# Another table of the issue order in a kernel of attention and MLP on one core

## The chip, the core and the metric

The kernel runs on one core of a Trainium2 chip. The metric is the device time of one launch in microseconds (us). A core has five engines with queues of their own, each working through its instructions in order: TensorE (PE, matrix products), VectorE (DVE), ScalarE (ACT), GpSimd (POOL) and SyncE (SP, which only issues transfers here). DMA transfers are issued by SP and ACT.

## The reference, cut

Four batches of eight heads with 768 tokens of 64 elements go through block-sparse attention (blocks of 32; a query block sees its neighbours, the first and the last block and three sampled ones; the first and the last query block see all). The result, 3072 tokens of 512, goes through an MLP with a width of 2048.

```python
mask = np.abs(blk_i - blk_j) <= window
mask = mask | (blk_i == 0) | (blk_j == 0) | (blk_i == n_blocks - 1) | (blk_j == n_blocks - 1)
...
scores = np.where(mask, scores, -1000000000.0)
scores = scores - np.max(scores, axis=-1, keepdims=True)
attn = np.exp(scores)
attn = attn / (np.sum(attn, axis=-1, keepdims=True) + 1e-09)
return np.matmul(attn, v).astype(np.float32)
...
h = x @ w_in
sp = np.where(h > 20.0, h, np.log1p(np.exp(np.minimum(h, 20.0))))
g = h * np.tanh(sp)
return (g @ w_out).astype(np.float32)
```

## The kernel before, in words

**Products.** Values of 32 bits are split into a high and a low part of 16 bits, and a product is the sum of three: high by high, high by low, low by high. In the listings `kt`, `q`, `v`, `ph`/`pl`, `xh`/`xl`, `wi`, `wo`, `g` and `sg` are such parts. Scales that keep the low parts in range come from sums of squares, which PE forms (`gram_k`, `gram_q`, `gram_v`, `gram_wi`, `gram_wo`, L373) and DVE reads off (L388).

**Attention.** A job is a group of 128 query rows by head pairs; job 0 is dense (first query block, `t_0_0` to `t_0_2`), jobs 1 and following read gathered blocks. For a job PE forms the scores `s` (L674), DVE their maximum `mx` (L737), ACT the exponentials `pt` (L756), PE transposes them (`t`, L680), ACT cuts the high part `ph` (L779), PE subtracts it (`t`, L787), ACT or DVE cut the low part `pl` (L792, L783), and PE multiplies by the values into `obank` (L818). DVE takes the reciprocal `r` (L837) and writes `xs`; PE transposes that (`tx`), and `xh`, `xl` are the MLP's input. Sampled blocks of k are copied to `kg` (ACT L608, POOL L611, DVE L615), whose places are read into registers first. Values are written to a DRAM buffer `vd` (L553) and gathered from there into one of three tiles `vg0` to `vg2` by DMAs on SP (the fixed blocks L571, the window L628, L631, the sampled blocks L635), with register loads for their places (L580) on SP ahead of them.

**Weights.** w_in comes in eight pieces of 1 MB (`wr_0` to `wr_7`) and w_out in sixteen of half that (`wor_0` to `wor_15`), all issued by one line, L893, on ACT's queue or on SP's. A piece is decoded by DVE in three steps (L901, L904, L907) out of one of three buffers, which come free when the third step is done, then scaled by its gram, and split into high (L962 on ACT, L965 on DVE) and low parts (L968).

**MLP.** For each of twelve tiles of 256 tokens PE forms `h` (L1068). ACT scales it to `hs` (L1079), takes exp (L1098), the square (L1104, or POOL L1103), ln (L1105) and exp (L1106); DVE puts a min/add (L1101) behind the first and a multiply (L1107) behind the last, which gives g. Its parts are cut by ACT or DVE (high, L1114, L1116) and POOL or DVE (low, L1120, L1122). The first tiles go through `y` (L1162). For the late tiles sums of parts (`us` by L1133, `sg` high L1144 on ACT or L1146, low L1148) replace some products (`yr`, L1281), and the results are put together in `yz` (L1314, L1320).

**Order.** All work is recorded as 2703 tasks, many with two ways (two engines). `Plan.emit` then reads the text table `ORDER` from left to right: a word is a task's number, a letter b takes its second way, and +n puts n zeros ahead of it, dummy products of PE on constants (`neg`, L1506). Since each engine works in order, the table sets the order of every engine and queue. A DMA carries one of eight completion semaphores (DMAHW0 to DMAHW7 in the listings), and it waits, at the head of its issuing engine's queue, until the transfer that had the semaphore before has landed, if that isn't known yet; it also waits for the buffer that it fills. What stands behind it on that engine waits with it.

Of the kernel before, what the change touches and what calls it, by code (L numbers as in the profile page):

```python
# [219 lines left out]
def attn_mish_kernel(ctx: ExitStack, tc: tile.TileContext, qT, kT, v, sampled, blocks, w_in, w_out, out):  # L220
# [1338 lines left out]
    147 97 72 183 55 179 98 112 341b 88 185 102 186 46 113 129 103+7 47 104 48 187 105 106 58 188+1 205 107 84 114 63  # L1559
    206 189 207 190+8 121 201 194 148 191 209+2 208 108 153 343+2 210 149 109 211 115 363 344 365b 195 340 116 196 345  # L1560
    122 213+4 212 130 197 217+7 150 203 214 131 135 123 346 215 124 110 216 348 347 342 154 125 367 132 198 352 126
    133 59 236 218 349 199 134 91 368 353 350+9 127 151 364 354 219 351 155 369 220+3 224 356 355 389 152 221 87 357
    156 370 222 366 387b 358 157 372+2 136 223 158 137 373 371 68 374+4 359 128 260b 244 391+2 80 375 138 360 411 421b
    361 419 392 166 83 139+3 159 362 388 376+3 140 393 225 160 377 226 141 394 378 142 237 143 396+2 261 65 245 380
    238 397 71 246 379 412 86 264 144 398 381 390 399 239 395 227 145 400+1 382 423 165 401 240b 247 228 70 383 443
# [3 lines left out]
    456 484 1629 268b 506 439 1638 457 440 485 257 486 235 1640 243 248 487 1630 488 253 441 164 458 442 489 459 482  # L1569
    510 1631b 254 1639 1641 511 529 1632 460 527 81 512 289 491 490 1651 500 492 285 78 1633 269 493 507 461 1652 513  # L1570
    249 1634 1642 290 514 515 258 494 286 462 495 1653 509 255 531 1643 270 1654 259 1635b 250 463 516 528 1655 1636
    496 501 517 518 532 1665 519 591 1656 272b 520 533 276b 497 1657 1644 291 292 89 521 251 498 522 1645 530 534 499
    293 523 1666 535 271 536 1668 1658 537 280b 273 1646 548 1659 538 524 1669 525 1667 526 1647 287 294 539 593 1660
    1679 1648 540 1680 1661 541 1649b 1662 551 1670 542 1650 552 1663b 543 1684 550 1671 549 544 1664 1685 553 1681
    554 295 1697 274 555 281 277 1698 275 1686 1672 464 1687 556 278 559 1702 279 560 557 561 1673b 296 282 297 298
    1688 299 1699 562 283 1674 300 1703 1689 558 563 1675 564 301 302 303 545 1717 1676 546 465 547 565 1704 304 1677
    466 1678 305 588 1718 306 467 566 590 307 1722 309b 1690 308 1723 310 1719 1691 313b 468 1735 311 469 314 1724 502
    1736 317 503 318 504 1740 312 321 1692 315 1682 1705 322 316 1683 325 505 470 1741 319 326 570 320 329 1695 323
    330 1696 324 333 589 327 334 592 567 1700 328 337 331 338 595 1725 332 1701 596 614 335 594 568 336 597 1713 598
    611 569 615 634 1714 599 612 90 1706 571 600 473b 1715 603 617 1716 604 613 601 1720 1707 618 572 602 619 1721 573  # L1580
    476b 605 620 606 1726 471 1733 616 1727b 477b 574 472 1734 621 575 607 1708 622 625 623 1693 1738 626 624 1694
    1728 627 1739 474 608 1729 576 478 628 1737 1751 629 609 610 475 630 1752 631 1709 632 1755 580 1753b 1710 1742
    1758 584 1730 1711b 585 640 636 635 1756 581 641 1712 1731b 1760 1743 582 1759 642 1757 665 659 577 586 1761 1754
# [18 lines left out]
    917 925 932 896 966 1924 1899 897 935 1928 967 926 1914 918 1915 1929 891 1900 919 898 1926 887 1916 888 976 968
    1930 920 1917b 1006 1901 981 1918 1902 947 1927 982 1931 957 977 983 1945 892 1009 1932 1946 893 984 1906 889 1950
    894 1919 948 890 1941 985 1000 1920 2303 986 989 987 1012 990 988 1933 969 1029 1031 991 1951 1947 1013 979 1028
    980 1934 992 949 1942 950 970 993 1315 1001 1032 994 1963 951 1935b 1943 1002 1964 1014 1003 1008 1015 2304 1948
    1016 2305b 1952 971 1017 972 1949 1004 973 978 1953 1961 1936 1954 1020 1921 1955b 1034 1011 1922 995 1035 1962
# [104 lines left out]
```

## Time and profile before

| what | value |
|---|---|
| time, median of 3 runs | 754.28 us (751.87 to 755.23) |
| profiled execution, its own time | 754.41 us |
| its span | 752.6 us |
| PE busy | 708.4 us (94%), mean granted clock 0.984 |
| ACT busy | 579.3 us (77%) |
| DVE busy | 548.1 us (73%) |
| POOL busy | 281.7 us (37%) |
| chain that ended last | PE 82%, DVE 7%, DMA 4%, issue 3%, SP's queue 2% |

The shares are means over the whole span. The page's slices of 1/40 show PE at half to eight tenths in the first six and at nine tenths behind them, so the stretch at the start has to be read by itself. "X <- Y" with a time means that the instruction X stood idle for that time and that Y was seen to end last of what it waited for.

### The profile page before, as it was taken

Reading aid. Unit: us, or ns where it says so; the run is one execution under the profiler, and the core shown is the slowest. Engines: PE = TensorE matmul, PEld = TensorE weight load, DVE = VectorE, ACT = ScalarE, POOL = GpSimd, SP = SyncE. Lnnn points to the kernel's source line nnn. Section 1 sums busy time; section 2 is a strip of 40 time slices with the busy share of each in tenths; the row PEclk is TensorE's granted clock in tenths of the full one; section 3 lists DMA queues with packets and bytes.
Section 4 is the critical chain, followed back from the end, with each engine's and each line's share of the span. In section 5 each row is a group of like instructions: output and inputs, shape, how many; then the busy total and the mean of one; then the engine's idle time right before and its main releaser. Section 6 shows DMA issues by size and latency. Waiting matters only on the chain.

```text
span 752.6 us, 31176 instructions
## 1 busy us (share of the span) xinstructions
PE 708.4 (94%) x13023; PEld 543.4 (72%) x13023; DVE 548.1 (73%) x1015; ACT 579.3 (77%) x927; POOL 281.7 (37%) x380
## 2 busy tenths in 40 slices
PE   5567798999999999999999999999999999999997
PEld 4455577875776776777676776677677778888887
DVE  5869878897667856977767757877886855577665
ACT  2648677999796788887877789886887786787783
POOL 2004234517754551244543454564374301200140
PEclk9889899999999999999999999999999999999999
DMA  8788766533235273247337353344532447000001
GB/s 302 249 250 245 227 212 179 198 121 88 108 112 167 83 251 103 93 132 217 91 104 229 102 213 108 82 142 144 159 88 72 145 131 245 16 1 15 16 29 43
DMA packets 60050, 103.75 MB, mean 138 GB/s; under 512 B 8579, under 2 KB 20868, under 8 KB 59908
## 3 DMA queue, kind: packets, MB, share of 16 engines
q1 hardware_dynamic: 54576, 88.90, 37.9%
q10 hardware_dynamic: 5332, 12.85, 5.2%
q8 instruction: 102, 1.67, 0.9%
q14 instruction: 40, 0.33, 0.1%
HBM read 84.58 MB, written 17.14 MB: 135 GB/s over the span
## 4 chain that ended last, share of the span: by engine, by line
PE 82%; DVE 7%; DMA 4%; issue 3%; SPq 2%; ACT 1%; POOLq 0%; ACTq 0%; POOL 0%; DVEq 0%
PE h_None L1068 31%; PE y L1162 21%; PE yr L1281 8%; PE obank L818 6%; PE t L680 6%; PE s L674 5%; DMA vg<-vd 2%; PE obank L1281 1%; PE tx L680 1%; DMA raw_k<-in_k_dram 1%; DVE hs_None L1107 1%; DMA raw_q<-in_q_dram 1%; SPq L580 1%; DVE v L504 1%; ACT pt L756 1%
## 5 line engine op out<-in xcount | busy, mean ns | idle before, releaser
L1068 PEld LDWEIGHTS <-wi 128*128 128x128 f16 x2304 | 223.8, 98 | 38.6 <-issue 5.4
L1068 PE MATMUL h_None<-xh,wi 128*128 128x256 f16 x1152 | 208.1, 274 | 3.2 <-issue 3.2
L611 POOL COPY kg<-kt 128x256 f16 x246 | 112.5, 491 | 163.2 <-PE s L674 146.3
L1162 PE MATMUL y<-wo,g 128*128 128x512 f16 x672 | 159.1, 379 | 0.0
L1068 PE MATMUL h_None<-xl,wi 128*128 128x256 f16 x576 | 157.6, 274 | 0.0
L1120 POOL TENSOR_TENSOR g<-hs_None,g 128x1024 f16<-128x1024 f32 x36 | 81.0, 2251 | 131.3 <-ACT g L1114 85.7
L1162 PEld LDWEIGHTS <-g 128*128 128x128 f16 x768 | 74.1, 98 | 70.8 <-issue 1.1
L756 ACT ACTIVATE pt<-s,nb,ns 128x256 f32<-128x256 f32 (+1 forms) x208 | 107.4, 584 | 1.3 <-DVE wi L907 0.9
L779 ACT ACTIVATE ph<-t 128x512 f16<-128x512 f32 x112 | 66.1, 600 | 47.1 <-PE t L680 39.2
L783 DVE SCALAR_TENSOR_TENSOR pl<-t,ph 128x512 f16<-128x512 f32 x99 | 67.0, 684 | 35.0 <-ACT ph L779 34.8
L680 PE MATMUL t<-ident,pt 128*128 128x128 f32 x448 | 68.9, 280 | 9.3 <-ACT pl L792 4.4
L1107 DVE SCALAR_TENSOR_TENSOR hs_None<-us_None,hs_None 128x1024 f32<-128x1024 f32 x48 | 62.7, 1307 | 18.9 <-ACT us_None L1106 17.6
L1079 ACT ACTIVATE hs_None<-h_None,gsc 128x512 f32<-128x512 f32 x96 | 66.0, 687 | 13.6 <-PE h_None L1068 13.6
L737 DVE TENSOR_REDUCE mx<-s 128x4 f32<-128x1024 f32 x44 | 53.7, 1220 | 27.8 <-PE s L674 27.8
L1068 PE MATMUL h_None<-xr,wi 128*128 128x256 f16 x576 | 67.8, 273 | 0.0
L680 PEld LDWEIGHTS t<-ident,pt 128*128 128x128 f32 x448 | 52.3, 143 | 21.3 <-ACT pl L792 5.7
L818 PEld LDWEIGHTS <-ph 128*32 128x32 f16 x3584 | 47.8, 94 | 14.7 <-issue 12.9
L1098 ACT ACTIVATE us_None<-hs_None,hsc 128x1024 f32<-128x1024 f32 x48 | 55.4, 1154 | 1.6 <-DVE sg L1148 1.1
L818 PE MATMUL obank<-vg,ph 128*32 128x65 f16 (+1 forms) x3200 | 49.1, 196 | 2.6 <-issue 2.3
L1105 ACT ACTIVATE us_None<-us_None 128x1024 f32<-128x1024 f32 x48 | 50.9, 1059 | 0.3
L1106 ACT ACTIVATE us_None<-us_None 128x1024 f32<-128x1024 f32 x48 | 50.7, 1060 | 0.4
L818 PEld LDWEIGHTS <-pl 128*32 128x32 f16 x1792 | 46.5, 96 | 5.7 <-issue 3.8
(258 smaller groups left out, 1202.9 us busy)
## 6 DMA issues: line engine op xcount, KB each, us to landing
vg<-vd SPq DMA_DIRECT2D x320, 65.0 KB, 2.6
vg<-vd SPq DMA_DIRECT2D x80, 195.0 KB, 3.2
wr<-in_moe_w_in_dram ACTq DMA_DIRECT2D x7, 1024.0 KB, 6.3
vd<-v SPq DMA_DIRECT2D x12, 520.0 KB, 4.2
vg<-vd SPq DMA_DIRECT2D x12, 520.0 KB, 5.3
raw_k<-in_k_dram SPq DMA_DIRECT2D x12, 512.0 KB, 5.8
raw_q<-in_q_dram SPq DMA_DIRECT2D x12, 512.0 KB, 4.4
raw_v<-in_v_dram SPq DMA_DIRECT2D x12, 512.0 KB, 4.9
```

Of the source, the lines that this page charges most:

```text
L611: nc.gpsimd.tensor_copy(out=dst, in_=tl["kt", b][:, :, ds(j, BS)])
L680: nc.tensor.matmul(out, src, ident, start=start, stop=stop, is_transpose=True)
L756: ex = lambda o, x, g, w: nc.scalar.activation(out=o, in_=x, func=AF.Exp, bias=nb[:, g, w:w + 1], scale=tl["ns", b, sus[w]["qb"] // TB][:, ...
L779: nc.scalar.activation(out=new(at_, "ph", ("ph", i, j), [P, 2, 2, P], F16), in_=tl["t", i, j], func=AF.Copy, scale=PSC)
L783: nc.vector.scalar_tensor_tensor(out=new(at_, "pl", ("pl", i, j), [P, 2, 2, P], F16), in0=tl["t", i, j], scalar=PSC, in1=tl["ph", i, j], o ...
L818: nc.tensor.matmul(o[cs, w, g, 0:v1 - v0], p[:, k, g, cs], vt[:, k, 2 * c + g, v0:v1], start=j == 0 and g == 0 and k == 0 and n == 0, stop ...
L1068: nc.tensor.matmul(h[:, f2, 0:n].rearrange("p (s q) -> p s q", q=BS), wi[:, fp, w, cc, fs], x[:, s0:s0 + sn, cc], start=f2 == 0 and k == 0 ...
L1079: nc.scalar.activation(out=tl[kq][:, 2 * (fp % 2):2 * (fp % 2) + 2, 0:n], in_=tl[kh][:, :, 0:n], func=AF.Copy, scale=gsc[:, fp:fp + 1])
L1107: add("DVE", 1.32 * c, lambda: nc.vector.scalar_tensor_tensor(out=hs(), in0=us(), scalar=-0.5, in1=hs(), op0=ALU.add, op1=ALU.mult), r=[ku ...
L1120: add("POOL", 2.3 * c, lambda: nc.gpsimd.tensor_tensor(out=g(1), in0=hs(), in1=g(0), op=ALU.subtract), r=[kq, ("gh",) + kp], w=[kp], use=[kg],
L1162: nc.tensor.matmul(tl[ky], tl["g", b, t, k][:, g, f, q], wo_at(fc)[:, w], start=fc == 0 and n == 0, stop=fc == NFC - 1 and n == 2)
L1281: nc.tensor.matmul(R(i), lhs, rhs, start=head and j == n == 0, stop=k == NFC // 4 - 1 and j == 1 and n == 2, skip_group_check=True)
```

## The change

Only the text of `ORDER` differs. It names the same 2703 tasks in another sequence; 128 of its words have the letter b (117 before), and 120 zeros stand at 16 places (113 at 22 before). The largest group of zeros, ahead of task 172 (the first transposes `t_0_0`), has 51 (33 before); of those that stood ahead of it, 5 and 6, none is left. 83 tasks change their engine: fifteen weight loads go from ACT's queue to SP's (seven of w_in, so that all eight are on SP, and eight of w_out) and one of w_out comes back; the high part of w_in's first piece goes from ACT to DVE; eleven squares go from ACT to POOL and seven the other way; seven casts of the early tiles' sums go from ACT to DVE and three back, five of g's high parts from DVE to ACT and three back, and some folds and copies of blocks change places in like numbers.

```diff
 ORDER = """
-    7 1 0 8 2 9 3 4 53 74 5 6 67 10 85 11 12 14 51 13 15 18 76 16 17 28 92 19 20 22 117b 29 21 61 24 23 75 30+5 93 77
-    99 25 49 54 27 31 32+6 167 26 69 33 34 38 202 64 39 168 192 42 35 56 52 118 169 170 36 119 37 171 60 94 43 62
-    172+33 120 176 57 173 66 174 44 111 175 82 200b 100 180 45 193 95 73 184 177 204 40 181 178 339b 182 96 41 50 101
...
+    7 1 0 2 3 5 8 4 9 10 67 11 12 51 13 14 6 18 60 15 117b 38 16 19 20 49 62 28 22 17 52 29 21 73 24 93b 23 58 30 77
+    99b 25 53 27 31 32 34 167 26 202b 33 118 192 200 168 92 35 61 59 42 119 169 69 43 79 36 39 120 170 37 94 111b 171
...
+    44 50 84 172+51 74 40 204 173 95 174 41 176 64 100 177 45 175 96 341b 180 193 101 147b 178 184 87 121 194 179 54
```

ACT's queue around the third score group, in the table of before. `wr_7` is a load of w_in, `ph_1_0` the high part of job 1's first transposed exponentials.

```order
L746 ACTIVATE nb_1_1133<-mx_1_1111,ns_0_0_277 128x4 [waits DVE_49]
L864 ACTIVATE xh_0_0_1135<-tx_0_1109 128x128 [waits PE_49]
L756 ACTIVATE pt_1_1138<-s_1_746,nb_1_1133,ns_0_0_277 128x256 [waits Activation_49]
L756 ACTIVATE pt_1_1138<-s_1_746,nb_1_1133,ns_0_0_277 128x256
L873 ACTIVATE xl_0_0_1136<-tx_0_1109 128x128 [waits PE_49]
L756 ACTIVATE pt_1_1138<-s_1_746,nb_1_1133,ns_0_0_277 128x256 x2
L893 DMA wr_7_1187<-in_moe_w_in_dram 128x4x512 [waits DMAHW2_49,DVE_49]
L779 ACTIVATE ph_1_0_1288<-t_1_0_1179 128x512 [waits PE_49]
L962 ACTIVATE wi_71<-wi_71,ws_0_1095 128x1024 [waits DVE_49]
```

The same place in the table of the change:

```order
L607 TENSOR_LOAD offk_86
L607 ISA x2
L608 ISA
L608 ACTIVATE kg1_114<-kt_0_230 128x8x32
L779 ACTIVATE ph_1_0_1360<-t_1_0_1159 128x512
L962 ACTIVATE wi_71<-wi_71,ws_0_1137 128x1024 [waits DVE_49]
L746 ACTIVATE nb_2_1410<-mx_2_1363,ns_0_0_285 128x4 [waits DVE_49]
L792 ACTIVATE pl_1_0_1413<-t_1_0_1159 128x512 [waits PE_49]
L873 ACTIVATE xl_0_0_1130<-tx_0_1124 128x128
L756 ACTIVATE pt_2_1428<-s_2_1183,nb_2_1410,ns_0_0_285 128x256 [waits Activation_49]
```

The load stands no longer ahead of `ph_1_0`; no DMA is left on ACT's queue until three loads of w_out, over 80 rows on. It now stands on SP. There, before, the rows from the fixed blocks of `vg2` to the first gathers of job 1's values:

```order
L571 DMA vg2_117<-vd0_60 32x1040
L580 TENSOR_LOAD offv_87
L580 ISA x2
L580 TENSOR_LOAD offv_87
L580 ISA x2
L580 TENSOR_LOAD offv_87
L580 ISA x2
L628 DMA vg0_115<-vd0_60 64x1040 [waits DMAHW4_49]
L631 DMA vg0_115<-vd0_60 32x1040 [waits DMAHW6_49]
```

and with the change:

```order
L571 DMA vg2_117<-vd0_60 32x1040
L893 DMA wr_7_1141<-in_moe_w_in_dram 128x4x512 [waits DMAHW5_49,DVE_49]
L580 TENSOR_LOAD offv_87
L580 ISA x2
L580 TENSOR_LOAD offv_87
L580 ISA x2
L628 DMA vg0_115<-vd0_60 64x1040 [waits DMAHW6_49]
L631 DMA vg0_115<-vd0_60 32x1040 [waits DMAHW7_49]
```

The load `wr_7` waits for a semaphore and a buffer, and the gathers into `vg0` stand behind it, with two register loads between them in place of three. `wr_2`, `wr_6` and `wr_4` come ahead of it on SP, and `wr_5` between the gathers into `vg0` and those into `vg1`.

At the end, ACT's last rows of the softplus of the last tile (numbers in names: batch, tile and piece, so that `us_3_2_3` is the last piece and `us_3_2_2` the one ahead of it), before:

```order
L1114 ACTIVATE g_3_2_2_19568<-hs_3_2_2_None_19404 128x1024
L1144 ACTIVATE sg_3_2_2_19599<-us_3_2_2_None_19433 128x1024 [waits DVE_49,PE_49]
L1104 ACTIVATE us_3_2_3_None_19552<-us_3_2_3_None_19552 128x1024 [waits DVE_49]
L1105 ACTIVATE us_3_2_3_None_19552<-us_3_2_3_None_19552 128x1024 [waits Activation_49]
L1106 ACTIVATE us_3_2_3_None_19552<-us_3_2_3_None_19552 128x1024 [waits Activation_49]
L1114 ACTIVATE g_3_2_3_19664<-hs_3_2_3_None_19521 128x1024 [waits DVE_49]
L1144 ACTIVATE sg_3_2_3_19689<-us_3_2_3_None_19552 128x1024 [waits DVE_49,PE_49,Activation_49]
```

and with the change:

```order
L1098 ACTIVATE us_3_2_3_None_19562<-hs_3_2_3_None_19521,hsc_81 128x1024 [waits DVE_49,Activation_49]
L1114 ACTIVATE g_3_2_2_19585<-hs_3_2_2_None_19379 128x1024 [waits DVE_49,PE_49]
L1105 ACTIVATE us_3_2_3_None_19562<-us_3_2_3_None_19562 128x1024 [waits Pool_49]
L1144 ACTIVATE sg_3_2_2_19615<-us_3_2_2_None_19456 128x1024 [waits DVE_49]
L1106 ACTIVATE us_3_2_3_None_19562<-us_3_2_3_None_19562 128x1024 [waits Activation_49]
L1114 ACTIVATE g_3_2_3_19665<-hs_3_2_3_None_19521 128x1024 [waits DVE_49,PE_49]
L1144 ACTIVATE sg_3_2_3_19690<-us_3_2_3_None_19562 128x1024 [waits DVE_49,Activation_49]
```

The square of `us_3_2_3` (L1104) has left ACT, for POOL, and the high part `sg_3_2_2` stands between its ln and its last exp. On DVE the min/add of `us_3_2_3` (L1101) comes ahead of the low part of `g_3_2_2`, not behind it, and the low part of `sg_3_2_3` comes ahead of that of `g_3_2_3`. PE uses `sg_3_2_3` two products of six instructions earlier than before, and `g_3_2_3` one later.

## Rows read from the trace of the kernel before

**Rows 1.** Windows: us, busy us (x instructions) of each engine, PEclk, DMA share, GB/s.
```profile
0.00:93.70 93.70, 61.72 (x1501) 48.06 (x1502) 70.99 (x163) 54.14 (x102) 18.73 (x38) 0.89 0.80 255
93.70:140.00 46.30, 42.86 (x1114) 36.42 (x1113) 36.17 (x65) 37.18 (x65) 21.32 (x28) 0.96 0.59 186
140.00:748.80 608.80, 603.84 (x10413) 458.89 (x10410) 440.47 (x788) 488.01 (x761) 241.65 (x316) 1.00 0.38 116
```

**Rows 2.** Timeline of PE: start us, us, instruction xcount, [idle us before <- releaser].
```profile
30.41 1.11 PE L680 MATMUL t<-ident,pt 128*128 128x128 f32 x4 [4.37 <-ACT pl L792]
...
51.97 0.53 PE L787 MATMUL t<-ph,neg 128*128 128x512 f16 x1 [4.18 <-ACT ph L779]
...
93.74 0.27 PE L1068 MATMUL h_None<-xh,wi 128*128 128x256 f16 x1
```

**Rows 3.** Waits of ACT from 18 to 60 us: us in total, times, longest us.
```profile
ACT ph L779 <- DMA vg<-vd: 4.6, 1, 4.6
ACT wi L962 <- DMA vg<-vd: 4.2, 1, 4.2
ACT pl L792 <- DVE wi L907: 4.1, 1, 4.1
```

**Rows 4.** Timeline of ACT (ACTq: issue on its queue).
```profile
50.87 0.40 ACTq L893 DMA_DIRECT2D wr<-in_moe_w_in_dram  x1
51.32 0.60 ACT L779 ACTIVATE ph<-t 128x512 f16<-128x512 f32 x1 [4.61 <-DMA vg<-vd]
```

**Rows 5.** Waits of DVE from 0 to 82 us.
```profile
DVE gram_wi L388 <- PE gram_wi L373: 6.4, 2, 4.2
DVE wi L901 <- DMA wr<-in_moe_w_in_dram: 3.2, 1, 3.2
```

**Rows 6.** Timeline of DVE: decode steps of w_in.
```profile
24.55 0.69 DVE L901 TENSOR_SCALAR wi<-wr 128x1024 int32<-128x1024 int32 x1 [3.18 <-DMA wr<-in_moe_w_in_dram]
...
43.67 1.21 DVE L907 SCALAR_TENSOR_TENSOR wi<-wr,wi 128x1024 int32<-128x1024 int32 x1
...
55.24 1.22 DVE L907 SCALAR_TENSOR_TENSOR wi<-wr,wi 128x1024 int32<-128x1024 int32 x1
```

**Rows 7.** DMA issues of the page: xcount, KB each, median us to landing.
```profile
vg<-vd SPq DMA_DIRECT2D x320, 65.0 KB, 2.6
...
wr<-in_moe_w_in_dram ACTq DMA_DIRECT2D x7, 1024.0 KB, 6.3
...
wr<-in_moe_w_in_dram SPq DMA_DIRECT2D x1, 1024.0 KB, 11.1
```

**Rows 8.** Timelines of ACT and of PE: a v copy, and the zeros.
```profile
23.97 1.16 ACT L500 ACTIVATE v<-raw_v,sc_v 128x1024 f16<-128x1024 f32 x1
...
19.47 3.56 PE L1506 MATMUL obank<-neg 128*128 128x240 f16 x33
```

**Rows 9.** Timeline of DVE: a split of w_out.
```profile
171.74 0.94 DVE L1025 SCALAR_TENSOR_TENSOR wo<-wo,cols 128x512 f16<-128x512 f32 x1
```

**Rows 10.** Timelines of SP (first gathers) and of PE (first product on vg).
```profile
41.28 0.63 SPq L628 DMA_DIRECT2D vg<-vd  x1
...
43.61 2.05 SPq L635 DMA_DIRECT2D vg<-vd  x3
...
56.13 0.25 PE L818 MATMUL obank<-vg,ph 128*32 128x65 f16 x8
```

**Rows 11.** Timelines of ACT, DVE and PE at the end; POOL's squares (min/median/max ns).
```profile
734.06 1.06 ACT L1104 ACTIVATE us_None<-us_None 128x1024 f32<-128x1024 f32 x1 [0.62 <-DVE us_None L1101]
...
741.35 1.23 DVE L1148 TENSOR_TENSOR sg<-us_None,sg 128x1024 f16<-128x1024 f32 x1
...
742.72 0.82 PE L1281 MATMUL yr<-wo,g 128*128 128x256 f16 x6
743.38 2.13 PE L1281 MATMUL yr<-to,sg 128*128 128x256 f16 x18
...
L1103 POOL TENSOR_TENSOR us_None<-us_None x16: 1889/1898/2807, 127.6 to 581.4; 128x1024 f32<-128x1024 f32 x16
```

More of the change, by code (lines that the diff above doesn't have):

```diff
@@ L1561 @@
[L1561 to L1565, printed above, removed]
[3 rows of a table removed]
@@ L1569 @@
[L1569 to L1583, printed above, removed]
@@ L1602 @@
[L1602 to L1606, printed above, removed]
@@ new lines @@
+    367 198 155 349 353 199 350 368 354 342 351 133 218 369 370 219 389 134 152 355 126 224b 387b 71 356+1 236b 220
+    364 136 372 221 156 222 373 223 374 137 357 375 260b 371 157+8 245 366 138 127 391+9 158 358 376 421b 392 419 75
+    139 68 359 140 411 225 377 128 78 393 378+7 86 360 380 379 226 361 390 394 237 141 142 362 381 261 143 227 396+3
+    246 288 397 159 388 382 395 412 160 398 144 400+1 399 423 401 238 145 240b 402 413 443 424 166 420 414+3 403 445
+    383 415 425 404 165 426 405 247 384 264b 262 427 428 228b 406 422 385 386 239 429 407+6 241 416 430 263 447 146
@@ new lines @@
+    1636 462 496 532 1665 1656 520 533 501 276b 287 1666 1644 1657 272b 251 290 497 534 1645 463 521 522 530 498 1668
+    535 523 499 1646 259 524 536 1658 525 1669 1647 271 280b 548 1659 526 537 291 1667 292 538 539 293 540 294 1679
+    591 1660 541 1648 551 1661 542 273 1649b 1662 543 549 1680 90 1670 1650 552 1663b 550 1684 1671 274 295 553 1685
+    1681 1664 544 554 1697 1686 277 555 1698 275 1672 1687 464 278 556 296 281 557 1702 1699 558 1673b 282 559 562
+    1688 560 1703 283 563 1674 1689 561 297 564 298 299 1675 300 545 565 279 1704 1676 465 301 590 302 303 1677 466
@@ new lines @@
+    2129b 2154 1376 2143 2330b 1312 2158 1395 1313 1377 1314 1359 1371 1337 1378 2159 1360 1345 1361 1392 2152 1394
+    2324 1362 1379 2130 2156 1363 1380 1397 1381 2155 1364 1414 1416 1382 1383 1398 1374 2173 1413 1399 1400 1338 2157
+    1365 1339 1393 1384 2144 2174 1385 2145b 1340 1417 1401 2169 1346 2134 2146 2325 1402 1366 2147 1419 1386 2175
+    1435 1420 1441 2326 2170 1396 2148 2160 1421 2178 1444 2171 1367 1422 1445 2179 1415 2327 1423 1403 2176 1368 1442
+    1404 1387 1405 2172 2177 1406 2180 1407 2161 1447 1408 2149b 1463 2162 2189 2181 1418 1464 1448 1466 1424 1427
@@ new lines @@
+    1480 2218 1529 1516 2230 1490 1481 2331b 1499 2332b 2233 1500 1517 1501 2231 2219 1530 2188 2202 1482 1518 1535
+    1519 2336 1502 1536 1579 2234 2237 1512 1503 1537 2203 2220 2235 1577 1483 1484 2204 1521 1531 2238 1522 1520 1538
+    2205 1504 2255 2206 1505 1539 1506 1509 1523 1540 2239 2236 2240 1576 1543 1541 2333 2241 2251 1544 2221 1542
+    2242b 1545 2252 2243 1554 2253 2244 1524 1555 2222 2256 1534 1580 1556 2260 2245 1557 1525 2258 2248b 2223 1558
+    2259 2224 2257 1559 1562 1582 1563 2337b 1560 1546 1564 1583 1565 1553 2274 1552 1584 2227 1566 1551 1601 2249
@@ new lines @@
+    2261 1585 2275 1598 1561 2228 1599 2276 2262 1602 1526 2277 1527 1547 2246 1567 2281 1586 1528 2247 1604 1568 2229
+    2278 2225 1587 1575 2282 2226b 2263 1574 2279 2338 1621 1588 2264 1573 2283 1605 2347 1589 1606 1581 2265b 1590
+    2280 2266 1548 1591 2348 1578 1549 1607 1550 1592 2350 2267 1569 2250b 1609 1600 1570 1610 2351 2349 1611 2284
+    2268 2366 1608 2285 1593 2271 2352 1612 1603 2367 1613 2269 1614 2373 1594 2270b 1595 2374 2254 2368 2295 2375
+    1571 1596 1572 2286b 1615 1597 2296 1616 2287 1617 2390 1618 2288 1619 1622 2339 2372 2272 2289 2340 2391 2342
@@ new lines @@
+    2341 2273b 2290 2345 2397 2344 2297 2376 2343 2291b 2346 2396 2364 2292 2398 2377 2392 2365 2293 2378 2371 2387
+    2370 2294 2379 2414 2380 2388 2353 2369 2381 2389 2354 2420 2382 2384b 2395 2355b 2415 2411 2435 2385 2413 2356
+    2394 2386 2438 2399 2393 2412 2400 2419 2357 2442 2401 2436 2383b 2402b 2418 2358 2416 2421 2403 2443b 2441 2361
+    2422 2444 2362 2437 2423 2440 2363b 2404 2453 2446 2359 2450 2454 2451 2424 2447 2456 2425 2448 2426b 2405 2417
+    2477 2360b 2406 2471 2457 2407 2455 2427 2439 2458 2495 2445 2408b 2428 2475 2452 2472 2429 2470 2430 2501 2476
@@ new lines @@
+    2409 2494 2473 2410b 2500 2432 2474 2478 2459 2525 2433 2460 2479 2461b 2434 2493 2462 2502 2518 2463 2480 2464
+    2519 2496 2431b 2465 2481 2467b 2526 2482 2524 2548 2483 2546 2497 2484b 2466b 2485 2547 2542 2468 2503 2549 2469b
+    2498 2499 2486 2523 2487 2504 2520 2505 2506 2521 2507 2527 2490 2508b 2522 2528 2509 2517 2510 2544 2491 2559
+    2511 2529 2492b 2541 2488 2560 2514b 2550 2530 2552 2543 2556 2553 2562 2554 2531 2577 2489b 2576 2599 2532 2561
+    2563 2515 2545 2533 2583 2551 2564 2516b 2581 2605 2565 2600 2578 2534 2566 2512 2607 2535 2582 2557 2536 2623
@@ new lines @@
+    2538 2558 2631 2449 2567b 2579 2513b 2568 2606 2537b 2569 2585 2580 2586 2539 2540b 2601 2587 2624 2588 2652 2602
+    2589 2570 2590b 2603 2591 2573b 2625 2604 2648 2592 2584 2609 2593 2574 2650 2575b 2594 2610 2596 2608 2611 2626
+    2612 2627 2597 2613 2595b 2571 2633 2655b 2614b 2598b 2630 2615 2653 2572b 2629 2616 2656 2632 2628 2651 2617 2634
+    2658 2657 2620 2669 2635 2668 2636 2675 2647 2637 2665 2662 2618 2638 2676 2672 2666 2619b 2639 2654 2621 2649
+    2663 2659 2673 2664 2640 2660 2667 2622b 2661 2674 2555 2298 2671 2641 2678 2642 2683 2644 2670 2677 2645 2679
@@ L1668 @@
+    2680 2646b 2685 2643b 2682 2687 2686 2691 2693 2689 2694 2690 2696 2681 2697 2700 2684 2698 2692 2699 2688 2701
+    2695 2702
 """
```

120 lines of the change are left out of this document (53 added, 67 removed), and 31 rows, old and new, of the table ORDER.

## The prediction

> **What bounds the kernel now.** I read the windows first: busy time of each engine in three stretches [rows 1]. From 140 us to 748.8 TensorE (PE) is busy for 603.84 of 608.80 us: it sets the pace there, and only 5.0 us are to be had. From 0 to 93.7 it is busy for 61.72 of 93.70, so it stands for 32.0 us, and for 3.4 us in the stretch between. The first MLP product, h, starts at 93.74 [rows 2]. So nearly all the time that an order of issue can give back lies before that product. In that stretch VectorE (DVE) is the busiest engine: 70.99 us of 93.70, with ScalarE (ACT) at 54.14.
>
> Next I read what the engines wait for there. ACT stands three times for over 4 us: 4.1, 4.2 and 4.6 [rows 3], 12.9 us in all. Each ends with a w_in load (L893) that ACT issues itself. The timeline shows the third: the load at 50.87 and, 0.45 later, the `ph` copy with 4.61 us of idle time ahead of it, put down to vg<-vd [rows 4]. The load waited for the completion semaphore that it shares with an earlier gather of SyncE (SP), and `ph`, which needed nothing of that load, stood behind it. PE then starts its `t` products 4.18 us late at 51.97, as it started the transposes 4.37 us late at 30.41 behind `pl` after the first hold [rows 2].
>
> DVE pays next: it waits 6.4 us in two waits (4.2 and so 2.2) for gram_wi, which stands in PE's order behind those late products, and 3.2 us for the first w_in load [rows 5]. That load, the only one issued by SP, took 11.1 us to land where ACT's seven took 6.3 in the median [rows 7]. DVE's three waits together: 6.4 + 3.2 = 9.6 us.
>
> **The change, part by part.** *Loads leave ACT's queue.* All eight w_in loads now stand on SP, and no DMA is issued by ACT between its first copies and three w_out loads, over 80 rows later. The three holds have no cause left on ACT. What passes on to the end isn't their 12.9 us but what the busiest engine loses by them: the 6.4 us of DVE's gram_wi waits. The 3.2 us should go too: the first load now leaves SP alone, with the next two behind it in the same queue, instead of sharing the engines with two of ACT's. It was issued 11.1 us ahead of DVE's start at 24.55 [rows 6], at 13.4; with some 6.3 it lands ahead of 20, and DVE wanted it at 24.55 − 3.18 = 21.4. **−9.6 us**; bounds 6.4 (the first load lands no sooner) and 12.9 (all of ACT's holds come through).
>
> *The same loads on SP.* Each issue costs SP about 0.40 [rows 4]. The critical place is the gathers of v blocks (vg), now behind wr_2, wr_6, wr_4 and wr_7. In the run of before the first gather group ends its issue at 43.61 + 2.05 = 45.66 and lands some 2.6 later [rows 10, 7], so at 48.3; the first product that reads it runs at 56.13 [rows 10]: 7.9 us to spare. Now that product is wanted 9.6 earlier, at 46.5. The gathers themselves start earlier by the 3.2 us that v's split no longer waits on DVE, and later by four issues, 1.6: ready at 46.7. That is even, so I take 0. wr_7 needs the buffer whose last decode ran on DVE from 43.67 to 44.88 [rows 6]; less the waits of 3.2 and 2.2 that is 39.5, and the gathers behind it, begun at 41.28 [rows 10] and moved by −3.2 + 1.6, would begin at 39.7: no hold by that either. If the cover is gone, this is where it costs; the rivals price it.
>
> *One high part of w_in moves from ACT to DVE* (L962 to L965). No row shows that operation on DVE; the nearest in size and kind is the decode's TENSOR_SCALAR of 0.69 us, with the decode's longer steps at 1.21 and 1.22 [rows 6]. DVE is the pace here: **+0.7**, bounds 0 (it falls into an idle moment of DVE) and 1.2.
>
> *Zeros and the first exponentials.* PE gets 51 zeros ahead of the first transposes instead of 33, but eleven fewer before; 33 took 3.56 us [rows 8], 0.108 each, so seven more are 0.8 us. ACT's last v copy, 1.16 us [rows 8], now stands ahead of the first `pt` and no longer behind, so these transposes come about 1.2 late. DVE has decode steps to do in that time, so I take 0 for both; 1.2 if this cover is gone.
>
> *Squares, casts and folds that swap engines* from 140 us to the tail (eleven squares leave ACT and seven come to it, the others in like numbers): the products and their number stay, and PE has 5.0 us of idle time there in all [rows 1], which other engines' waits cause. I take 0, with 3 us either way as a bound: some of that idle time found, or as much again lost. Between the start and this stretch stands a second gate: the last of the first splits of w_out on DVE, at 171.74 [rows 9], which PE's first y products read. It moves up with DVE's work; the 0.7 counted above is the only thing that DVE gains on the way to it.
>
> *The tail.* In the order of before the last `g` low part stands ahead of the last `sg` low part on DVE, which runs 741.35 to 742.58; PE uses `g` at 742.72 and `sg` six products into the group that starts at 743.38, at 744.03 [rows 11]. Now `sg` is used two groups of 0.66 earlier, at 742.72. Ahead of it the last square goes from ACT to GpSimd (POOL): 1.90 us in place of 1.06 [rows 11], so +0.84; a high part of `sg` (also 1.06) now stands between the last two exponentials; and one min/add step of DVE is put one 1.23 us operation earlier. 742.58 + 0.84 + 1.06 − 1.23 = 743.25: PE waits 0.5. The `g` low part, now behind it on DVE, comes 1.2 later and costs some 0.6 more. **+1.1**, bounds 0 and 3 (the two added operations in full, 1.9, and a DVE operation more).
>
> Sum on the profiled execution, 754.41 us (span 752.6 and 1.8 around it; the median of the runs is 754.28, so the two can be read as one): 754.4 − 9.6 + 0.7 + 1.1 = **746.6 us**.
>
> **Rivals.** *A: the hold only moves to SP, no change.* SP issues in order too. If wr_4 and wr_7 hold it as they held ACT, 4.2 + 4.6 = 8.8 [rows 3], the first gather is ready at 46.7 + 8.8 = 55.5 where the product wants it at 46.5: 9.0 of the 9.6 are gone, 754.4 − 9.6 + 9.0 + 1.8 = 755.6. For: the load still waits for a decode and a semaphore. Against: the gathers that ACT's loads waited for now stand behind the load, and the decode is done by 39.5. On this side lies also that ACT's own time was all that was lost: it gets back an issue of 0.40 for each load, off the path, and other work ends late at the same places, 754.4 + 0.7 = 755.1. Against that stand the 4.61 us that ACT stood ahead of `ph` [rows 4], ten times the issue.
>
> A page states a rule that gives this second form. The Trainium skill, DMA: Bandwidth & Descriptors, section "Issuing engines are not separate DMA queues", says that starting DMAs from several engines saves only the issuing sequencer's time, usually small beside the transfer. By that rule the move of fifteen loads to SP and one back is worth 14 × 0.40 = 5.6 us of an engine that isn't the pace, and the sum would be 755.1; the row of 4.61 us disagrees, since what ACT lost was a wait and not an issue.
>
> *B: more.* All of ACT's holds come through at PE, since DVE's later work is free to follow: 754.4 − 12.9 = 741.5, with the 0.7 and the 1.1 hidden. For: PE's waits of 4.37 and 4.18 [rows 2] follow ACT, not DVE. Against: DVE is busy for 70.99 of 93.70.
>
> *C: slower.* SP is held for the last w_in load as well. wr_5 stands ahead of the second gather group and needs the decode that ran from 55.24 to 56.46 in the run of before [rows 6]; moved 9.6 up it ends at 46.9. If DVE isn't earlier, wr_5 goes at 56.5, the gathers follow, O and r follow them, and DVE's next decode follows r: a loop that repeats at each load. Price: all three holds, 12.9, in SP's line where nothing covers them: 754.4 − 9.6 + 12.9 + 1.8 = 759.5. It decides where wr_5's decode comes later than about 50 us.
>
> **How the numbers follow.** Forecast 0.57: its mechanism stands in rows of three engines. B 0.11, A 0.18 (0.04 of it in its second form), C 0.14. The predicted time is the forecast's, 746.6; its own range, by the bounds (−12.9 to −6.4; 0 to +1.2; +1.2 for the first exponentials; 0 to +3; ±3), most of which won't fall on one side together, is about 741 to 751. The range for 8 in 10 reaches from B less a little to A and a little over: 740 to 757, and leaves C and its like out. The bounds of faster and slower lie 0.5% (3.8 us, about what a measurement of this kernel can tell from no change) from 754.28: 750.5 and 758.1. Forecast and B are faster, 0.68; A is the same, 0.18; C is slower, 0.14.
>
> **What would show it.** The first h product at 84 to 86 us instead of 93.74; no idle time of ACT over 2 us between 24 and 52; no gram_wi wait of 4 us on DVE; the first decode on DVE with no wait for wr; the first product on vg at 46 to 47 and no wait of PE for vg<-vd. Wrong would be: PE or DVE waiting for vg<-vd or for a wr load (A, C); h at 81 with DVE idle (B); or an early h whose gain is gone by 748, which would put the loss into the stretch that I took at 0. In the tail PE should wait once or twice, about 1 us in all, for `sg` and `g`.

## The result and the profile after

| kernel | median | runs | ratio to before, fast runs, 95% interval |
|---|---|---|---|
| before | 754.16 us | 12 (749.57 to 757.51, and one of 829.04) | |
| changed | 745.47 us | 12 (742.29 to 751.02) | 0.9897 (0.9872 to 0.9923) |

The ratio leaves out the run of 829.04 us, which is over 1.5% above the fastest. By the ratio the change is faster by 1.03%, 7.8 us of 754.2; 746.6 us was forecast for its time. Its profiled execution took 744.38 us, with a span of 742.6 where before's was 752.6. Two runs of one program lie up to 9 us apart, so a trace is one draw; this bears on much of what follows.

The windows of the changed kernel, with the columns of [rows 1]:

```profile
0.00:93.70 93.70, 64.83 (x1700) 51.84 (x1702) 76.16 (x168) 58.57 (x111) 19.73 (x41) 0.91 0.83 265
93.70:140.00 46.30, 44.85 (x1038) 39.66 (x1021) 40.73 (x74) 41.36 (x70) 24.33 (x25) 1.00 0.69 221
140.00:738.80 598.80, 594.25 (x10321) 451.97 (x10318) 428.91 (x770) 478.80 (x742) 254.83 (x325) 1.00 0.37 114
```

From 93.7 to 140 us PE stands for 1.4 us where it stood for 3.4, at a granted clock of 1.00 (2.4 GHz) where the mean was 0.96. What changed most stands at the start. PE's first product on gathered values and its first h product, against 56.13 in [rows 10] and 93.74 in [rows 2]:

```profile
49.72 0.25 PE L818 MATMUL obank<-vg,ph 128*32 128x65 f16 x8
...
88.71 0.27 PE L1068 MATMUL h_None<-xh,wi 128*128 128x256 f16 x1
```

The three holds of ACT in [rows 3] are gone. Its largest waits from 18 to 60 us (us in total, times, longest) are nearly all for products and maxima that it needs itself:

```profile
ACT kg L608 <- PE s L674: 3.5, 1, 3.5
...
ACT nb L746 <- DVE mx L735: 1.7, 1, 1.7
ACT ph L779 <- PE t L680: 1.7, 2, 1.1
```

DVE's waits of [rows 5] shrink too: gram_wi has 1.2 us for 6.4, and the first weight load none for 3.2 (the first decode starts at 18.50 without a wait; the 1.4 us below are for a later load, at 39.20). A new wait of 3.0 us comes in:

```profile
DVE tp_w L407 <- PE tp_w L396: 3.0, 1, 3.0
...
DVE wi L901 <- DMA wr<-in_moe_w_in_dram: 1.4, 1, 1.4
DVE gram_wi L388 <- PE gram_wi L373: 1.2, 1, 1.2
```

On SP the load `wr_7` goes at 41.05, 1.6 us ahead of the first gathers, and `wr_5` at 46.19 ahead of the next ones. No load stands long enough for PE to miss a gather by more than 1.1 us:

```profile
41.05 0.38 SPq L893 DMA_DIRECT2D wr<-in_moe_w_in_dram  x1
42.63 0.63 SPq L628 DMA_DIRECT2D vg<-vd  x1
...
44.11 1.98 SPq L635 DMA_DIRECT2D vg<-vd  x3
46.19 0.53 SPq L893 DMA_DIRECT2D wr<-in_moe_w_in_dram  x1
```

What DVE's 3.0 us wait for is PE, and PE there waits for nothing that the profile shows ("issue"). First the changed kernel from 44 to 88 us, then before from 44 to 94:

```profile
PE tp_w L396 <- issue: 3.1, 1, 3.1
PE s L674 <- issue: 2.6, 2, 2.3
PE obank L818 <- issue: 1.6, 1, 1.6
...
PE obank L818 <- issue: 3.3, 2, 2.1
...
PE s L674 <- issue: 0.2, 1, 0.2
```

These are 7.3 us, 3.8 more than before's 3.5. A lead that is 8.4 us at 60 us (the table below) is 5.0 at the first h, 3.4 less. Where these waits come from shows further down.

### The profile page after: what moved, and what is told of

It is laid out like the page before. It is cut to its first block, busy times and chain, and to the rows that moved or that the text cites. A ratio compares the mean times of both kernels' runs of the same rounds, so it can differ in the third digit from the quotient of the medians.

```text
span 742.6 us, 31198 instructions
## 1 busy us (share of the span) xinstructions
PE 703.9 (95%) x13030; PEld 543.5 (73%) x13030; DVE 546.3 (74%) x1011; ACT 578.7 (78%) x921; POOL 298.9 (40%) x390
## 4 chain that ended last, share of the span: by engine, by line
PE 80%; DMA 7%; DVE 5%; ACT 3%; SPq 3%; issue 2%; ACTq 0%
PE h_None L1068 29%; PE y L1162 21%; PE yr L1281 8%; PE obank L818 6%; PE t L680 6%; PE s L674 5%; DMA vg<-vd 2%; DMA raw_q<-in_q_dram 2%; PE obank L1281 1%; PE tx L680 1%; DMA wr<-in_moe_w_in_dram 1%; SPq L580 1%; SPq L635 1%; ACT pt L756 1%; DMA raw_k<-in_k_dram 1%
## 5 line engine op out<-in xcount | busy, mean ns | idle before, releaser
L611 POOL COPY kg<-kt 128x256 f16 x246 | 111.0, 487 | 156.5 <-PE s L674 146.7
L1120 POOL TENSOR_TENSOR g<-hs_None,g 128x1024 f16<-128x1024 f32 x34 | 75.9, 2235 | 101.3 <-ACT g L1114 68.0
L1107 DVE SCALAR_TENSOR_TENSOR hs_None<-us_None,hs_None 128x1024 f32<-128x1024 f32 x48 | 59.6, 1244 | 19.7 <-ACT us_None L1106 17.5
L1103 POOL TENSOR_TENSOR us_None<-us_None 128x1024 f32<-128x1024 f32 x20 | 40.4, 2021 | 76.6 <-DVE us_None L1101 76.6
L1101 DVE TENSOR_SCALAR us_None<-us_None 128x1024 f32<-128x1024 f32 x48 | 36.6, 763 | 27.4 <-ACT us_None L1098 27.4
L1105 ACT ACTIVATE us_None<-us_None 128x1024 f32<-128x1024 f32 x48 | 50.9, 1060 | 2.2 <-POOL us_None L1103 1.9
```

Source lines behind the costliest of these rows:

```text
L611: nc.gpsimd.tensor_copy(out=dst, in_=tl["kt", b][:, :, ds(j, BS)])
L1107: add("DVE", 1.32 * c, lambda: nc.vector.scalar_tensor_tensor(out=hs(), in0=us(), scalar=-0.5, in1=hs(), op0=ALU.add, op1=ALU.mult), r=[ku ...
L1120: add("POOL", 2.3 * c, lambda: nc.gpsimd.tensor_tensor(out=g(1), in0=hs(), in1=g(0), op=ALU.subtract), r=[kq, ("gh",) + kp], w=[kp], use=[kg],
```

## The experiments

Beside the times I compare **leads**: PE's tasks have the same work in every kernel, so for each trace I add up, task by task, the least time that any of the traces shows for that task, and ask when each kernel had done as much of it as before had at a given time. The lead is how much earlier that was (worked out from all rows of PE, one profiled execution each). Every time stands beside runs of before on the same chip: e1 to e4 ran on one chip, e5 to e8 on a second, e9 to e12 on a third.

```
us in the run of before     30    60  93.7   140   200   450   700
changed                    1.8   8.4   5.2   9.0   9.0   7.8  10.1
changed, once more (e11)   1.3   8.6   9.0   6.4   6.4   4.6   6.9
before, w_in loads on SP   3.3   7.9   2.8   4.2   4.2   2.4   2.1   (e1)
before, all its loads so   3.6   8.7   1.3   2.3   2.3   1.5   1.9   (e5)
changed, w_in on ACT       0.4   4.0   1.4   2.4   2.3   2.2   4.3   (e2)
changed, loads as before   0.5   3.5   4.9   6.0   6.0   3.6   5.1   (e6)
changed until first h      1.6   9.3   4.0   3.9   3.0   2.7  -0.1   (e3)
changed from first h on   -0.2  -0.4   0.7   3.5   3.4   1.8   3.7   (e4)
changed until 190 us       0.2   7.8   8.9   8.3   8.3   6.4   3.7   (e8)
the same, 5 zeros fewer    1.2   8.7   4.6   5.2   5.2   4.0   2.3   (e9)
before, 6 zeros more      -0.1   0.2  -0.6   2.2   1.6  -0.6  -2.8   (e10)
```

The theory of the prediction, called H: what the change removes are ACT's holds behind its own weight loads. Rival A: the holds move to SP. Rival R: the new sequence gains by itself, whichever queue has the loads. A fourth, F, came up on the way.

### The loads' queue alone

e1 gives the seven w_in loads of the table of before to SP, at their places; e5 gives every load the queue that the changed table gives it.

```diff
-93 99 111 129 135 147 153
+93b 99b 111b 129b 135b 147b 153b
```

> The table of before with one edit: the seven w_in loads that ACT issued are issued by SP at the same places of the table. Theory H (ACT's holds behind its loads are what the change takes away): ACT's three idle times of 4.1 to 4.6 us go, DVE's gram_wi waits shrink from 6.4 to under 2, the first h comes 4 to 9 us earlier, time 746 to 750. Rival A (the hold only moves to SP): the first gathers start 4 us or more later than at 41.28, PE waits for vg<-vd, time 752 to 757. Rival R (the new sequence, not the queue, is what gains): ACT's idle times go but the first h stays within 2 us of 93.74, time 752 to 756.

Measured: 0.9964 (0.9935 to 0.9994), 752.05 us beside 755.10, a third of the change. No theory came out whole. ACT's three holds go and DVE's gram_wi waits shrink to 0.6 us, as H has it, and the first gathers start at 39.64, not later as A has it; but the time is none that H allows. The lead at 60 us is 7.9, nearly all that H wants; at the first h (90.94) it is 2.8. ACT's timeline shows a part of where it went: the next DMA on its queue, a load of w_out, holds it as the others had.

```profile
55.50 0.36 ACTq L893 DMA_DIRECT2D wor<-in_moe_w_out_dram  x1
55.90 1.08 ACT L779 ACTIVATE ph<-t 128x512 f16<-128x512 f32 x2 [3.80 <-DMA vg<-vd]
```

So the hold stands one DMA further on, and by H e5 should have kept the lead.

> The table of before, but every weight load on the queue that the changed table gives it: seven loads of w_in and eight of w_out go from ACT to SP, one of w_out comes back; the sequence stays. In the trace of the kernel with the w_in loads alone moved, ACT stood for 3.8 us behind its next DMA, a load of w_out. Theory H (any DMA on ACT's queue in the start holds it): that wait goes too, the first h is at 87 to 90, time 746 to 750. Rival A (the holds go over to the gathers on SP): PE waits more for vg<-vd, time 751 to 756, as with the w_in loads alone or worse.

Measured: 0.9965 (0.9938 to 0.9992), 753.26 beside 757.30: no better. The time lies in rival A's range, but not by A's way: the first gathers start at 40.41, ahead of before's 41.28, and PE has no wait for vg<-vd over 0.15 us from 30 to 94. No DMA holds ACT any more, and the lead at 60 us is 8.7; then the first h comes at 92.4. The rows of SP, DVE and PE, and of SP's waits from 30 to 62 us the longest in e5 and the same one in before:

```profile
41.88 4.62 SPq L635 DMA_DIRECT2D vg<-vd  x3
46.60 0.41 SPq L893 DMA_DIRECT2D wr<-in_moe_w_in_dram  x1
...
54.50 1.59 DVE L901 TENSOR_SCALAR wo<-wr 128x1024 int32<-128x1024 int32 x1 [3.29 <-DMA wr<-in_moe_w_in_dram]
...
57.49 1.03 PE L373 MATMUL gram_wi<-wi 128*128 128x128 bf16 x8 [5.17 <-DVE wi L907]
...
SPq L635 <- DMA wr<-in_moe_w_in_dram: 5.3, 3, 2.7
...
SPq L635 <- DMA wr<-in_moe_w_in_dram: 1.9, 1, 1.9
```

On SP the gathers wait for the landing of earlier w_in loads. `wr_7` stands behind the gathers on SP and goes at 46.60 (at 41.05 in the changed kernel); it lands 7.9 us later, DVE stands 3.29 us for it at 54.50 with other decode steps behind, and PE 5.17 us ahead of its product at 57.49. The hold had changed its queue, as A says, but what it delays is the next w_in load and not a product on gathered values.

### The sequence alone

e2 gives the seven w_in loads of the changed table back to ACT, e6 gives all loads the queues of before; the sequence stays the changed one.

```diff
-93b 99b 111b 129b 135b 147b 153b
+93 99 111 129 135 147 153
```

> The changed table with one edit: the same seven w_in loads go back to ACT's queue, at their places in the changed table. Theory H: ACT stands again in holds of several us at wr_4, wr_7 or their like, the first h falls back from 88.71 to 92 to 97, time 750 to 756. Rival R: the sequence has placed the loads where they don't hold, first h within 2 us of 88.71, time 744 to 748.

> The changed table, but every weight load on the queue that the table of before gives it; the sequence stays. Theory H: ACT is held by loads of w_in and of w_out, first h at 92 to 97, time 750 to 756. Rival R (the new sequence gains by itself): 744 to 749.

Measured: e2 0.9910 (0.9872 to 0.9947), e6 0.9895 (0.9846 to 0.9944). The intervals are wide (7 and 6 runs), but both lie near the change's 0.9897 and clear of 1: by time R is right and H is not. The loads' queue adds nothing to the new sequence that these runs can tell. The first h comes at 92.60 and 89.30. The holds are there, but smaller. Of e6, ACT's two longest ahead of a load up to 60 us:

```profile
44.10 0.38 ACTq L893 DMA_DIRECT2D wr<-in_moe_w_in_dram  x1
44.53 1.02 ACT L756 ACTIVATE pt<-s,nb,ns 128x256 f32<-128x256 f32 x2 [3.15 <-issue]
...
51.23 0.38 ACTq L893 DMA_DIRECT2D wr<-in_moe_w_in_dram  x1
51.65 0.30 ACT L746 ACTIVATE nb<-mx,ns 128x4 f32<-128x4 f32 x1 [1.65 <-DVE wi L968]
```

In all they are 5.4 us in e6 (0.18, 0.43, 3.15, 1.65) and 4.9 in e2, where before had 14.2 up to 57 us. With the new sequence alone ACT is held less for its loads; the queue then takes the rest. In the leads at 60 us the queue counts for more: 8.4 and 8.6 for sequence and queue, 7.9 and 8.7 for the queue alone, 3.5 and 4.0 for the sequence alone. But what is kept is decided behind 60 us. By 93.7 us the old sequence with the loads on SP gives back 5.1 and 7.4 us (e1, e5), the new one with them from nothing (e11, e8) to 5.3 (e3). Which part of the new sequence keeps the gain isn't shown; no run takes it apart.

### Where in the program the gain lies

e3 takes the changed sequence for what before issues ahead of its first h, and before's for the rest; e4 is the reverse.

```diff
 ORDER of e3: the words of the changed table that stand in
 7 1 0 8 2 ... 432+4 429      (before's table ahead of 1623)
 then before's table from 1623 on
```

> The changed table's sequence for everything that before puts ahead of the first h product, then before's sequence for the rest. If all of the gain is made at the start: 744 to 748. If it is made half at the start and half behind the first h, as the two profiles read (lead 5.0 us at the first h, 10.0 at the end): 748 to 751, with a half-clock stretch and a gap of PE of about 2 us near 115.

> The reverse: before's sequence up to the first h, then the changed table's. If all of the gain is made at the start: 752 to 756. If half of it is made behind the first h: 748 to 751. The tail is the changed one here: by the term of the tail in the prediction PE waits about 1 us for sg and g at the end; by the profile of the changed kernel it doesn't wait.

Measured: 0.9983 (0.9958 to 1.0009) and 0.9979 (0.9950 to 1.0007). Neither half gains by itself what can be told from nothing, though the whole change has 1%. e4's time is the one expected if all of the gain is made at the start, but e3's is in neither range. e3 has a lead of 9.3 at 60 us and has none at 700. A cut at the first h also leaves 8 of 337 tasks on the wrong side, so e8 cuts at 190 us, where the two tables have all but 3 of 744 tasks in common.

> The changed table's sequence for all that before issues ahead of PE's work at 190 us, then the sequence of before: both sequences have nearly the same tasks behind them there. If the gain lies in the first 190 us and the rest is worth 0, as predicted: 744 to 748, the tail as before. If the tail of the change costs 1.1 us as predicted: 743 to 747. If the late region carries some of the gain: 748 to 752.

Measured: 0.9965 (0.9931 to 0.9998), 753.94 beside 757.30. Its start is that of the change (first h at 85.04, lead 8.3 at 200 us), and 4.6 of this goes between 200 and 700 us, in stretches where every engine's sequence is that of before. By the expectation a time so short of the change's would mean that the late region carries some of the gain; the trace tells it another way. The rows show gaps of PE with no release, the longest of them in the middle of a row of equal small products:

```profile
554.55 0.21 PE L818 MATMUL obank<-vg,pl 128*32 128x65 f16 x3
556.72 0.19 PE L818 MATMUL obank<-vg,pl 128*32 128x65 f16 x1 [1.96 <-issue]
...
PE obank L818 <- issue: 5.6, 4, 2.0
```

The sum of all gaps over 0.9 us behind 200 us, from start to start of PE's products, is 11.4 us (9 gaps) in e8 and 3.5 (3) in before. The page has a queue for instructions, q8 (packets, MB, share):

```profile
q8 instruction: 102, 1.67, 0.9%
```

These are 102 packets of 16 KB. The trace of before has 26,176 instructions on PE's queue (13,023 products, as many weight loads, 130 semaphore instructions), so a packet goes to about 256 of them. The place of the waits fits that. Counted from 0 along PE's queue, each of the 139 waits of PE over 0.15 us that the profile puts down to issue, behind 10 us and in all fourteen traces, begins 193 or 194 instructions past a multiple of 256. The 80 of them over 0.6 us end 1.2 to 1.75 us after the end of a q8 packet. Of the 57 gaps over 0.9 us behind 200 us in the fourteen traces, 34 stand at such a place; the other 23 have a release by another engine or a transfer. So PE stands there for the next packet of its own program. Theory F takes this one step further: which instructions stand at these places decides how long PE waits there.

The waits ahead of the first h are of the same kind: the 3.1, 2.3 and 1.6 us of the changed kernel stand at such places.

### Moving PE's instructions

e8's program for PE stands 11 instructions further along behind 190 us than before's, by zeros and semaphore instructions. e9 takes five zeros away ahead of the first transposes, and stands 1 further along; e10 adds six to the table of before, in a wait of 4.18 us, and stands 12 further along.

```diff
-172+51
+172+46
```

```diff
-211
+211+6
```

> The kernel of the changed table until 190 us and the sequence of before behind it, with one edit: five zeros fewer ahead of the first transposes (46 for 51). In the profile of the kernel with 51, PE loses some 5 us behind 200 us in gaps that name no release and that end 1.3 to 1.5 us after a 16 KB packet of the instruction queue; its PE program stands 11 instructions further along there than that of before, and with 46 zeros it stands 1 further along. Theory F (which instructions a fetch begins with, and so what PE and the DMA engines do when it is due, decides on those gaps): the gaps behind 200 us shrink to before's 3 to 5 us in all, time 746 to 750. Rival L (the sequence of before behind 190 us loses a lead whatever the place of its instructions): gaps as with 51 zeros, 8 us or more, time 751 to 755.

> The table of before with six more zeros, in PE's wait of 4.18 us ahead of the product at 51.97 (0.65 us of zeros, hidden there): only the place of PE's later instructions moves, by 12. Theory F: the gaps behind 200 us grow from 3.5 us to 7 to 12, time 757 to 762 where before is near 755. Rival L: gaps as in before, time within 2 us of before.

Measured: e9 0.9887 (0.9859 to 0.9915), 745.32 beside 753.93; its interval lies clear of e8's. With five dummy products fewer the ratio is 0.8% lower, and the program with before's sequence behind 190 us is as fast as the changed one. The two ran on different chips; the ratio of another program, the changed table without zeros, was 0.4% higher on e9's chip than on e8's (e12, e7 below), so the chip doesn't explain it as far as these runs tell. e10 1.0033 (1.0009 to 1.0057), 756.58 beside 753.93: slower by 2.5 us by the ratio (0.7 to 4.3), just within the 2 to 7 us over before that F expected, with 0.65 us of zeros that lie in a wait. By time alone rival L, within 2 us, isn't excluded; by the gaps it is. PE's issue waits behind 200 us (us in total, times, longest), of e10 and then of before:

```profile
PE obank L818 <- issue: 5.9, 4, 1.9
...
PE h_None L1068 <- issue: 3.2, 4, 1.0
...
PE obank L818 <- issue: 0.5, 2, 0.3
```

All gaps over 0.9 us there: 7.9 us (5) against 3.5 (3). Twelve instructions further along, the waits fall mostly on the small products `obank`, as in e8, and not on `h`. For e10 time and trace go together. For e9 they don't quite: its gaps are 8.5 us (7) against e8's 11.4, on h now,

```profile
PE h_None L1068 <- issue: 4.2, 4, 1.4
PE obank L818 <- issue: 1.0, 3, 0.5
```

but its profiled run was the slowest of its six (752.11), with a first h at 89.65. That e10's twelve instructions cost time is measured. How much of e9's some 6 us comes from these waits is not shown: its trace has 1.8 us less of them than e8's.

The lost leads of all kernels that have before's sequence behind 200 us go along with these waits. Of issue waits behind 200 us before has 4.0 us; e5, e9, e1, e3, e10 and e8 have 0.7, 1.9, 2.4, 2.4, 3.6 and 3.7 more, and from 200 to 700 us they lose 0.4, 2.9, 2.1, 3.1, 4.4 and 4.6 us of their leads. So the profiled runs of e1 and e3 hold some 2.4 us of such waits beside what they test, and small differences between the kernels should be read with that much doubt. e1 and e5, with the same order of tasks on PE, differ by 1.7 us in them. That PE waits for its packets is thus shown; that the place of the instructions decides how long, and not the run, rests on the times of e10 and e9.

### The zeros, and the control

> The changed kernel once more, as the control on this chip and for a second profile: 743 to 748 and a first h within 2 us of 88.71 if its profile stands for its runs; if the start varies from run to run by several us, the first h comes elsewhere between 84 and 92 while the time keeps to 743 to 751.

> The changed table without its 120 zeros, the dummy products of PE. If they only fill waits and do nothing for the clock: within 1 us of the changed kernel, 744 to 748. If they keep PE's clock up in the waits: longer stretches at a granted clock of 0.50 before 90 us than the changed kernel's four, and 747 to 753. If they stand in the way of work: 740 to 744.

> The changed table without its 120 zeros, beside the changed kernel on one chip: if the zeros are worth nothing, both within 2 us of each other; if they cost, this one is 2 to 4 us faster.

```diff
-172+51
+172
 (and so at the other 15 places: 120 zeros fewer)
```

Measured: e11, the change once more, 0.9884 (0.9852 to 0.9916), 745.75 us. Without zeros 0.9872 (0.9829 to 0.9916) in e7, and 0.9910 (0.9881 to 0.9939), 747.49 us, in e12 beside e11. The zeros are worth nothing that these runs can tell. In the trace of e12 PE's clock is granted at 0.50 (1.2 GHz) for some 34 of the first 92 us, in those of e7, the same program, and e11 for some 17 (from windows of 2 us); the spans of e12 and e7, 744.1 and 743.9, are the same all the same. The control's first h, and its issue waits from 44 to 85 us:

```profile
84.92 0.27 PE L1068 MATMUL h_None<-xh,wi 128*128 128x256 f16 x1
...
PE s L674 <- issue: 1.6, 2, 1.0
...
PE obank L818 <- issue: 0.8, 1, 0.8
```

The same program has its first h at 88.71 in one run and at 84.92 in the other, with spans of 742.6 and 745.8: the start varies by 4 us from run to run, and the later stretch takes it back or not. The issue waits ahead of it differ alike, 7.3 and 2.4 us. So they do in e12 and e7, again one program: 6.5 and 2.1 us, with the first h at 88.78 and 84.89. The order of tasks sets where PE can run out of instructions, and one run and the next differ in how long it stands there.

## Why the prediction came out

**What bounds: right.** PE sets the pace from 140 us on (594.25 of 598.80 us busy), and the gain lies ahead of that: the lead of the changed kernel is 9.0 at 140 us and 10.1 at 700, and that of its second trace 6.4 and 6.9.

**−9.6 for the loads: about right at 60 us, wrong as the cause of the gain.** ACT's holds went, DVE's gram_wi waits went from 6.4 to 1.2 us and its wait for the first load from 3.2 to none, with 1.4 for a later one; at 60 us every kernel of the table with these loads on SP leads by 7.8 to 9.3 us. But I let this run through to the end by itself. e1 and e5 show that it doesn't: with the old sequence the queue alone is worth 0.35%, 2.7 us. And e2 and e6 show that the new sequence has about 1% with the loads on ACT. I read the change as the move of the loads and took the reordering of the first 90 us as 0; it is the step that failed, though the sum hides it. The two together remove the holds (14.2 us of ACT, then 4.9 to 5.4, then none), and the new sequence also has `wr_7` ahead of the gathers on SP, where the old one has it behind them. That these two things are how the new sequence gains is likely, but not shown.

**The gathers on SP: 0, about right, with wrong times.** The first product on them ran at 49.72, not at 46.5; PE waited 1.1 us once for vg<-vd, at 58.12.

**The first h at 84 to 86: once right, once wrong,** 84.92 and 88.71. A price that I didn't have stands there: PE's waits for its own instructions, 7.3 us in the first trace and 2.4 in the second, where before has 3.5. The order of tasks doesn't tell how long they are.

**+0.7 for the split on DVE: right as its duration,** 0.74 at 42.41 (L964, the same statement). No run shows what it costs in time.

**Zeros and first exponentials, 0: right** for the zeros by e7 and e12. That the first exponentials come later shows in the leads at 30 us (1.8 for 3.3 to 3.6 with the old sequence), and is gone by 60.

**From 140 us on, 0 with 3 either way: right by both traces of the change,** whose leads grow by 1.1 and 0.5 us from 140 to 700, and by the time of e9, which has before's sequence there and the change's time. The bound was too small for e8, which loses 4.6.

**The tail, +1.1: wrong, it is 0.** The rows of ACT, DVE and PE that answer to [rows 11], and behind them the last exp and ln of before:

```profile
719.23 1.15 ACT L1098 ACTIVATE us_None<-hs_None,hsc 128x1024 f32<-128x1024 f32 x1
...
723.11 1.06 ACT L1105 ACTIVATE us_None<-us_None 128x1024 f32<-128x1024 f32 x1 [0.93 <-POOL us_None L1103]
724.08 1.04 ACT L1144 ACTIVATE sg<-us_None 128x1024 f16<-128x1024 f32 x1
725.02 1.04 ACT L1106 ACTIVATE us_None<-us_None 128x1024 f32<-128x1024 f32 x1
...
730.91 1.23 DVE L1148 TENSOR_TENSOR sg<-us_None,sg 128x1024 f16<-128x1024 f32 x1 [1.18 <-ACT sg L1144]
732.05 1.22 DVE L1122 TENSOR_TENSOR g<-hs_None,g 128x1024 f16<-128x1024 f32 x1
...
731.41 0.82 PE L1281 MATMUL yr<-to,g 128*128 128x256 f16 x6
732.07 1.47 PE L1281 MATMUL yr<-to,sg 128*128 128x256 f16 x12
733.38 0.82 PE L1281 MATMUL yr<-wo,g 128*128 128x256 f16 x6
...
729.24 1.15 ACT L1098 ACTIVATE us_None<-hs_None,hsc 128x1024 f32<-128x1024 f32 x1
...
735.15 1.06 ACT L1105 ACTIVATE us_None<-us_None 128x1024 f32<-128x1024 f32 x1
```

PE's groups follow each other at 0.66 us with no gap. `sg_3_2_3` is ready at 732.14 and `g_3_2_3` at 733.27, just ahead of their uses (732.73 in the group at 732.07, and 733.38). I had the two added operations right, but not what the min/add's earlier place is worth: ln starts 3.88 us after the exp here (719.23 to 723.11), where in before the square started 4.82 after it (729.24 to 734.06) and ln 5.91 (735.15). That step is 2.0 us earlier although POOL's square takes 1.9; I had it 0.4 earlier.

So the sum came to within 1.1 us of the median in part by luck: the first term is right where it was read, but it held to the end only in the new sequence, which I had at 0 and which by time has the gain without it.

**Rivals.** A happened in the old sequence (e5) as far as that the hold moved to SP, with the cost at the next w_in load and not at the gathers. B didn't: the lead never came to 12.9. C didn't: `wr_5` went at 46.19, ahead of its limit of 50. What none of them held is R, that the new sequence gains by itself, and F.

## What to carry to other kernels

A DMA on a compute engine's queue costs what stands behind it, not its issue: look for idle time of the engine that ends with the load, and ask both whether the load can go to another queue and whether it can go to a place where its buffer is free, and test the two apart. Here the other queue alone kept a third of the gain, and the new order alone, with the old queues, kept all of it that the times can tell. An edit that leaves every engine's sequence alone can still move the time through the place of the instructions in the program (0.33% for e10, up to 0.8% between e8 and e9), so an effect of that size needs a control that moves them without doing anything else. And where a profile shows "issue", count the instructions along that engine's queue before looking for a cause in the order.

## What the runs showed of the hardware that I had not expected

PE's waits "for issue" of up to 4 us are waits for its own program: all 139 over 0.15 us in fourteen traces begin 193 or 194 instructions past a multiple of 256, the number that one 16 KB packet of the instruction queue goes to, and the 80 over 0.6 us end 1.2 to 1.75 us after such a packet. Twelve instructions more ahead of them made the same sequence 0.33% slower (0.09 to 0.57%); ten fewer went with 0.9887 of before where 0.9965 had been measured. And the two runs of one program put the first h 3.8 us apart, with 7.3 and 2.4 us of such waits ahead of it, without a like difference at the end.
